# A new order, a float32 fetch and six magnitudes on ScalarE in a fused attention and MLP kernel

## The chip, the cores and the metric

The kernel runs on one core of a Trainium2 chip. A core has five engines that work side by side and meet through semaphores: TensorE (PE; PEld is its loading of weights), VectorE (DVE), ScalarE (ACT), GpSimd (POOL) and SyncE (SP). POOL, SP and ACT can also start transfers (DMAs); what they start runs on 16 shared DMA engines. POOL's transfers can change the type on the way (float32 in memory, bf16 on chip); the transfers that SP and ACT start here move bytes as they are. The metric is device time in microseconds (us) of one launch. The kernel before took 396.82 us (median of three runs, 396.26 to 397.13).

## The reference: what is computed

Eight batches, eight heads, 576 positions, 64 numbers a head, all float32. Every head does masked attention; the first four heads look at the last 32 positions ("local", L in the code), the other four at the positions that are the same modulo 32 ("strided", S). The outputs of all heads stand side by side as 512 numbers for each of 4608 tokens and go through an MLP whose activation is a rational function.

```python
scores = q @ k.T / sqrt(64)
scores = where(mask, scores, -1e9); attn = softmax(scores)
x = (attn @ v) as [4608, 512]
h = x @ w_in                                   # [4608, 2048]
P = a[0] + a[1]*h + a[2]*h**2 + a[3]*h**3
Q = 1 + abs(b[0])*abs(h) + abs(b[1])*h**2
out = (P / (Q + 1e-6)) @ w_out                 # [4608, 512]
```

## The kernel before, in words

Everything on chip is bf16, sums of matmuls are float32 in PSUM, whose eight banks are shared out.

**Attention** goes batch by batch (function `attention`), each in four steps: L heads, S heads, S heads, L heads. A step is: scores on PE, the row maximum on DVE (L805, L887), its subtraction by one more matmul, exp on ACT (L818, L900), a transpose of the result, the product with v on PE (L848, L943), and the division on DVE (L859, L953). Then `turn` transposes the batch's output into XT, which ACT copies out of PSUM (L765). q and k must be transposed too. For batches 0 and 1 (`b < NPE`), `casts` fetches q and k on POOL's queue with conversion to bf16 into an MLP buffer h (L560; two halves n = 0 and n = 1 for L and S heads, q and k each: four transfers a batch), and `loads_pe` transposes them on PE (L623, L660); ACT copies q out of PSUM, DVE copies k (L642 to L674). For batches 2 to 7, POOL writes bf16 copies of q and k to memory, and SP's transposing transfers bring them in; the results of exp are transposed by SP's transfers too (L836, L920).

**The MLP** goes in nine chunks of 512 tokens. `mlp1` makes the 2048 columns of h in two groups of eight tiles: four matmuls a tile (L980), an ACT copy from PSUM into the group's h buffer (L986). Then the activation works on the whole group, 4096 numbers in each of 128 partitions. On DVE, one after the other: z = |h| by clearing the sign bits (L1023), u = b1 z + b0 (L1025), u = u z (L1027). On ACT: u = exp(-ln(u + 1.000001)), the reciprocal of Q (L1051, L1053). On DVE: z = a3 h + a2 (L1054), z = z h (L1056), z = z + a1 (L1057), z = z h (L1058), z = z + a0 (L1059), h = z u (L1060). The first group of chunk 0 is cut in halves (L1003 to L1013), the last group of chunk 8 in smaller pieces, with its magnitude and one step made by ACT (L1019, L1020). `mlp2` multiplies with w_out (L1086), copies out (L1098) and stores (L1105). There are five h buffers, two z and two u buffers, used in turn.

**The order of the work** is not the order of the code. Every operation is recorded with its engine, an assumed duration, a key and the tiles it reads and writes. `schedule` then plays the program forward: at each moment, each engine that is free takes, of the operations whose inputs are ready by the assumed durations, the one with the lowest key. The result is one fixed list for each engine, with semaphore waits between the engines. Keys are in units of tokens: attention of batch b has b*576 and up, the MLP of chunk c has c*512 plus an offset. `QUOTA` says how many PSUM tiles of each kind may be open at once ("ph" are those that the MLP's first matmuls and small transposes write). Where PE would idle at the start or the end, the planner puts in matmuls whose result nobody reads (`filler`, L136). A transfer is assumed to land 2.2 us after its turn, and 9 us later still when it starts after 60 us.

In the planner, an engine is free again when an operation's duration is over, and what depends on it on the same engine can follow at once:

```python
free[e] = t + o.dur
...
lat = 0.0 if u.eng == o.eng else 0.15
u.ready = max(u.ready, o.fin + lat)
```

Of the kernel before, what the change touches and what calls it, by code (L numbers as in the profile page):

```python
# [12 lines left out]
ACT_SET_ID = 6  # L13

# [70 lines left out]
class Prog:  # L85
    QUOTA = {"at": 3, "ph": 3, "sm": 2, "po": 4}
# [64 lines left out]
    def schedule(self):  # L151
# [69 lines left out]
        while left:  # L221
# [45 lines left out]
            for u in o.users:  # L267
                lat = 0.0 if u.eng == o.eng else 0.15
# [101 lines left out]
def bass_strided_sparse_attn__then__act_rational_pade_kernel(nc, q, k, v, moe_w_in, moe_w_out, moe_a, moe_b, out):  # L370
# [7 lines left out]
    HL = H // 2  # L378
# [93 lines left out]
    for dst, srcc in ((IDN, id_c), (ML, ml_c), (MS, ms_c)):  # L472
# [4 lines left out]
         0.1, -1e5, w=[T_co], dma=0.1)  # L477
    P.op("sp", lambda e: e.dma_start(coef[:, 0:4], bass.AP(tensor=pa.tensor, offset=pa.offset, ap=[[0, 128], [1, 4]])),
         0.1, -1e5, w=[T_co], dma=0.1)
    P.op("sp", lambda e: e.dma_start(coef[:, 4:6], bass.AP(tensor=pb.tensor, offset=pb.offset, ap=[[0, 128], [1, 2]])),  # L480
         0.1, -1e5, w=[T_co], dma=0.1)
    T_b.new()
    P.op("dve", lambda e: e.scalar_tensor_tensor(coef[:, 6:8], coef[:, 4:6], -1.0, coef[:, 4:6],
                                                 op0=Alu.mult, op1=Alu.max), 0.2, -1e5, r=[T_co], w=[T_b])
# [58 lines left out]
    def casts(b, after=None):  # L543
        after = after if after else [()] * 7
        key = b * 576 - 1500 if b > 1 else -1e5 + 3e4 * b
# [3 lines left out]
        for n in range(2):  # L549
# [3 lines left out]
            for i, (s_t, d_t, t) in enumerate(((q, q16, T_q[b][n]), (k, k16, T_k[b][n]))):  # L553
# [3 lines left out]
                if b >= NPE:  # L557
                    bulk(s_t, d_t, b, HL * n, HL, H, t, key, after[3 * n + i])
                    continue
# [46 lines left out]
    def loads_pe(b, key, tq, tk, after):  # L606
        for n in range(2):
            h = stage[b, n]
            hv = h.t[:, :, :].rearrange("p g c -> p (g c)")
            for i, (t, st_) in enumerate(((tq, T_q[b][n]), (tk, T_k[b][n]))):  # L610
# [14 lines left out]
                P.op("pe", tr, 1.0, key + 2 * n, r=[st_, h, T_c], w=[sl], after=after)  # L625
# [37 lines left out]
                P.op("pe", tr2, 0.7, key + 1, r=[st_, h, T_c], w=[sw], after=after)  # L663
# [14 lines left out]
    def loads(b, after=(), pace=None):  # L678
        g0, g1, g2 = [[pace[i]] for i in range(3)] if pace else [()] * 3
        key = b * 576 - 20 if b else -700  # L680
# [53 lines left out]
    def turn(b, kind, src, key):  # L734
        for kk in range(2):
# [16 lines left out]
            P.op("pe", tr, 0.5, key, r=[src, T_c], w=[sm])  # L752
# [15 lines left out]
    def attention(b, st):  # L768
# [5 lines left out]
        for kind, idx in (("L", 0), ("S", 0), ("S", 2), ("L", 1)):  # L774
            key = base + 144 * u
# [3 lines left out]
            if kind == "L":  # L779
# [3 lines left out]
                def score(e, tq=tq, tk=tk, sc=sc, idx=idx):  # L783
# [19 lines left out]
                P.op("pe", score, 1.15, key, r=[T_c] + st["TL"], w=[sc])  # L803
# [3 lines left out]
                    1.2, key, r=[sc], w=[ng])  # L807
# [8 lines left out]
                P.op("pe", negm, 0.5, key, r=[ng], m=[sc])  # L816
# [5 lines left out]
                if b < NPE:  # L822
                    for j in range(2):
# [8 lines left out]
                        P.op("pe", trp, 0.5, key, r=[pp, T_c], w=[ph])  # L832
# [20 lines left out]
                P.op("pe", av, 0.8, key, r=[pt] + st["vlr"], w=[acc])  # L853
# [13 lines left out]
            def score(e, tq=tq, tk=tk, idx=idx, sc=sc):  # L867
# [17 lines left out]
            P.op("pe", score, 1.0, key, r=[T_c] + st["TS"], w=[sc])  # L885
# [3 lines left out]
                0.85, key, r=[sc], w=[ng])  # L889

            def negm(e, ng=ng, sc=sc):
# [6 lines left out]
            P.op("pe", negm, 0.4, key, r=[ng], m=[sc])  # L898
# [3 lines left out]
                0.75, key, r=[sc], w=[pp])  # L902
            pt = R_ptS.next()
            if b < NPE:
                for j in range(2):
# [10 lines left out]
                    P.op("pe", trp, 0.4, key, r=[pp, T_c], w=[ph])  # L916
# [31 lines left out]
            P.op("pe", av, 0.5, key, r=[pt, vS], w=[acc])  # L948
# [3 lines left out]
            for x in range(2):  # L952
# [5 lines left out]
                    0.66, key, r=[acc, rc], w=[xsb])  # L958
            if idx:
                turn(b, "S", xsb, base + 500)  # L960
        turn(b, "L", xl, base + 550)
        return land

    def mlp1(c):
        xt = cur_xt[c]
        xc = CH * (c % 3)
        base = c * CH + 1500 if c else 1000
        groups = []
        for g in range(NG):
            h = R_h.next()  # L970
            cut = c == 0 and g == 0
            hf = [Tile(f"hf{i}") for i in range(2)]
            for f in range(g * G, g * G + G):
                ph = PTile("ph", 1)
                key = base + f * 16
# [7 lines left out]
                o = P.op("pe", mm, 0.9, key, r=[xt, T_win[f // G]], w=[ph], after=h.prev)  # L983
                if f == 7:
# [3 lines left out]
                     0.6, key, r=[ph], w=[h, hf[f % G // 4]])  # L988
            key = base + 256 + g * 256
# [7 lines left out]
            def dv(fn, dur, **kw):  # L997
                P.op("dve", fn, dur, key, **kw)
# [16 lines left out]
            else:  # L1015
                if end:
# [4 lines left out]
                         3.7, key, r=[h, T_co], w=[y])  # L1021
                else:
# [33 lines left out]
            dv(lambda e, zz=zz, hh=hh: e.tensor_tensor(zz, zz, hh, op=Alu.mult), tt, r=[h], m=[z])  # L1056
            dv(lambda e, zz=zz: e.tensor_scalar(zz, zz, a_ap[1], None, op0=Alu.add), ts + 0.22, m=[z])  # L1057
            dv(lambda e, zz=zz, hh=hh: e.tensor_tensor(zz, zz, hh, op=Alu.mult), tt, r=[h], m=[z])  # L1058
# [116 lines left out]
```

## Time and profile before

| | |
|---|---|
| runs, us | 397.13, 396.26, 396.82 |
| profiled run, us | 396.87 |
| its span (first to last instruction), us | 395.1 |
| mean granted clock of TensorE | 0.982 |
| matrix multiplications and weight loads | 3859 each |
| DVE instructions | 324 |
| ACT instructions | 316 |
| DMA traffic | 45.76 MB |

A line of the profile names a group of instructions by the kernel's line (L1023 is line 1023), the engine, the operation, what it writes and reads (out<-in) and the shapes; after the bar stand busy us, mean ns of one instruction, and how long the engine was idle just before it and for whom. In the timeline the first number is the start in us, the second the length, and square brackets show idle time before it and what ended it. Instructions of one kind in a row are merged (x2, x16). In a table by stages each engine has its busy time in that stretch and its number of instructions. "SPq" is SP's queue of DMA issues. A matmul's end in the trace is modelled, so PE's busy time is not PE at its peak.

### The profile page before, as it was taken

The page shows a single profiled execution, that of the slowest core. Times are in us where ns is not written, and L with a number is a line of the kernel's source. Part 1 is how long each engine was busy: PE and PEld are TensorE (multiplying, and loading weights), DVE is VectorE, ACT ScalarE, POOL GpSimd, SP SyncE. Part 2 cuts the span into 40 slices and gives each one's busy share as a digit, 9 for nine tenths or more (in the row PEclk, how much of TensorE's full clock was granted, in tenths as well). Part 3 has the DMA queues.
Part 4 walks back from the last instruction along what each step waited for, and adds up shares of the span by engine and source line. Part 5 has one row for each costly group of instructions (what it writes and reads, how often), then busy time and mean ns, then how long its engine had stood idle before and what let it go on. Part 6 is the DMA issues. An engine that isn't in the chain of part 4 may idle for free.

```text
span 395.1 us, 8720 instructions
## 1 busy us (share of the span) xinstructions
PE 358.1 (91%) x3859; PEld 174.5 (44%) x3859; DVE 360.7 (91%) x324; ACT 290.9 (74%) x316; POOL 102.5 (26%) x136
## 2 busy tenths in 40 slices
PE   6889878989999999689989999999899999899695
PEld 2564545344544454344434544444354344344242
DVE  4673999999998999959999999999999999999995
ACT  1356896869387875848696979597968796899971
POOL 8993000640290049004801720001000100101100
PEclk9699999989999999999999999999999999999999
DMA  7999999999599659999999999205300200200202
GB/s 103 175 206 173 215 150 114 122 143 196 161 133 162 129 142 124 124 102 192 141 148 231 146 179 205 51 28 143 60 2 27 81 0 28 81 0 2 106 0 106
DMA packets 129094, 45.76 MB, mean 116 GB/s; under 512 B 116832, under 2 KB 125280, under 8 KB 128864
## 3 DMA queue, kind: packets, MB, share of 16 engines
q0 software_dynamic: 68864, 27.99, 56.8%
q1 hardware_dynamic: 60192, 17.22, 30.6%
q8 instruction: 30, 0.49, 0.5%
q14 instruction: 8, 0.07, 0.1%
HBM read 39.29 MB, written 16.52 MB: 141 GB/s over the span
## 4 chain that ended last, share of the span: by engine, by line
DVE 64%; PE 21%; DMA 7%; issue 4%; ACT 3%; POOL 0%; SPq 0%; POOLq 0%
DVE z L1056 8%; PE PSUM L980 8%; DVE u L1027 8%; DVE h L1060 7%; PE PSUM L1086 7%; DVE z L1058 7%; DVE u L1025 5%; DMA ptS<-pS 5%; DVE z L1057 5%; DVE z L1054 4%; DVE z L1023 4%; DVE z L1059 4%; DVE xS L953 3%; DMA h<-in_q_dram 2%; DVE ng L805 2%
## 5 line engine op out<-in xcount | busy, mean ns | idle before, releaser
L980 PE MATMUL PSUM<-XT,Win 128*128 128x512 bf16 x576 | 135.9, 381 | 12.4 <-ACT h L986 4.5
L1086 PE MATMUL PSUM<-Wout,h 128*128 128x512 bf16 x576 | 135.3, 382 | 6.0 <-DVE h L1060 5.9
L986 ACT ACTIVATE h<-PSUM 128x512 bf16<-128x512 f32 x144 | 82.9, 599 | 40.9 <-PE PSUM L980 40.7
L980 PEld LDWEIGHTS PSUM<-XT,Win 128*128 128x128 bf16 x576 | 51.0, 98 | 80.4 <-ACT h L986 16.5
L1086 PEld LDWEIGHTS PSUM<-Wout,h 128*128 128x128 bf16 x576 | 54.4, 98 | 69.7 <-DVE h L1060 5.8
L1051 ACT ACTIVATE u<-u,consts 128x4096 bf16<-128x4096 bf16 x16 | 59.3, 3709 | 13.1 <-DVE u L1027 12.7
L1105 POOL DMA_DIRECT2D out_dram<-os x32 | 20.9, 656 | 182.5 <-ACT os L1098 182.5
L1053 ACT ACTIVATE u<-u 128x4096 bf16<-128x4096 bf16 x16 | 57.9, 3620 | 0.3
L1027 DVE TENSOR_TENSOR u<-u,z 128x4096 bf16<-128x4096 bf16 x17 | 39.0, 2291 | 0.5
L1058 DVE TENSOR_TENSOR z<-z,h 128x4096 bf16<-128x4096 bf16 x17 | 38.9, 2291 | 0.5
L1056 DVE TENSOR_TENSOR z<-z,h 128x4096 bf16<-128x4096 bf16 x17 | 38.9, 2287 | 0.4
L1060 DVE TENSOR_TENSOR h<-z,u 128x4096 bf16<-128x4096 bf16 x17 | 38.8, 2283 | 0.4
L573 POOL DMA_DIRECT2D vL<-in_v_dram x32 | 27.4, 886 | 0.0
L1098 ACT ACTIVATE os<-PSUM 128x512 f32<-128x512 f32 x34 | 19.2, 605 | 10.8 <-PE PSUM L1086 10.5
L524 POOL DMA_DIRECT2D q<-in_q_dram x6 | 5.3, 888 | 83.9 <-DMA tk<-k 83.9
L765 ACT ACTIVATE XT<-PSUM 128x576 bf16<-128x576 bf16 (+2 forms) x40 | 19.4, 563 | 9.8 <-PE PSUM L749 6.0
L1025 DVE TENSOR_SCALAR u<-z,coef 128x4096 bf16<-128x4096 bf16 x17 | 22.8, 1344 | 0.5
L953 DVE TENSOR_TENSOR xS<-PSUM,rc 100x512 bf16<-100x512 f32 x32 | 20.5, 683 | 2.9 <-PE PSUM L943 2.6
L1057 DVE TENSOR_SCALAR z<-z,coef 128x4096 bf16<-128x4096 bf16 x17 | 22.3, 1312 | 0.5
L1059 DVE TENSOR_SCALAR z<-z,coef 128x4096 bf16<-128x4096 bf16 x17 | 21.8, 1280 | 0.3
L1054 DVE TENSOR_SCALAR z<-h,coef 128x4096 bf16<-128x4096 bf16 x16 | 21.7, 1354 | 0.4
L1023 DVE TENSOR_SCALAR z<-h 128x4096 uint16<-128x4096 uint16 x16 | 19.5, 1220 | 2.4 <-ACT h L986 2.4
(87 smaller groups left out, 388.4 us busy)
## 6 DMA issues: line engine op xcount, KB each, us to landing
out_dram<-os POOLq DMA_DIRECT2D x32, 256.0 KB, 3.6
q<-in_q_dram POOLq DMA_DIRECT2D x12, 288.0 KB, 8.0
k<-in_k_dram POOLq DMA_DIRECT2D x12, 288.0 KB, 9.1
vL<-in_v_dram POOLq DMA_DIRECT2D x32, 96.0 KB, 10.5
vS<-in_v_dram POOLq DMA_DIRECT2D x16, 144.0 KB, 10.1
Win<-in_moe_w_in_dram POOLq DMA_DIRECT2D x8, 256.0 KB, 12.6
Wout<-in_moe_w_out_dram POOLq DMA_DIRECT2D x4, 512.0 KB, 23.9
h<-in_q_dram POOLq DMA_DIRECT2D x4, 288.0 KB, 13.5
```

The costliest lines, as they stand in the source:

```text
L980: r = e.matmul(ph.f, Win[:, kk, f * 128:(f + 1) * 128], XT[:, kk, xc:xc + CH], start=(kk == 0), stop=(kk == NK1 - 1))
L986: P.op("act", lambda e, f=f, ph=ph, h=h: e.activation(h.t[:, f % G, :], ph.f, AF.Copy), 0.6, key, r=[ph], w=[h, hf[f % G // 4]])
L1025: dv(lambda e, zz=zz, uu=uu: e.tensor_scalar(uu, zz, b1_ap, b0_ap, op0=Alu.mult, op1=Alu.add), ts + 0.28, r=[z, T_b], w=[u])
L1027: dv(lambda e, zz=zz, uu=uu: e.tensor_tensor(uu, uu, zz, op=Alu.mult), tt, r=[z], m=[u])
L1051: P.op("act", lambda e, uu=uu: e.activation(uu, uu, AF.Ln, bias=eps1, scale=1.0), 0.833 * W / 1000 + 0.28, key, r=[T_co], m=[u])
L1053: P.op("act", lambda e, uu=uu: e.activation(uu, uu, AF.Exp, scale=-1.0), 0.833 * W / 1000 + 0.19, key, m=[u])
L1056: dv(lambda e, zz=zz, hh=hh: e.tensor_tensor(zz, zz, hh, op=Alu.mult), tt, r=[h], m=[z])
L1057: dv(lambda e, zz=zz: e.tensor_scalar(zz, zz, a_ap[1], None, op0=Alu.add), ts + 0.22, m=[z])
L1058: dv(lambda e, zz=zz, hh=hh: e.tensor_tensor(zz, zz, hh, op=Alu.mult), tt, r=[h], m=[z])
L1059: dv(lambda e, zz=zz: e.tensor_scalar(zz, zz, a_ap[0], None, op0=Alu.add), ts + 0.22, m=[z])
L1060: dv(lambda e, zz=zz, hh=hh, uu=uu: e.tensor_tensor(hh, zz, uu, op=Alu.mult), tt, r=[z, u], m=[h])
L1086: r = e.matmul(po.f, h.t[:, j, m * 128:(m + 1) * 128], Wout[:, kk, :], start=(kk == 0), stop=(kk == NF - 1))
```

## The change: what it does

1. *The planner's model.* A VectorE operation keeps its engine for 0.083 us less than its duration, an ACT operation for 0.11 less (`OVER`); an operation that depends on one of the same engine is ready 0.035 (DVE) or 0.03 us (ACT) after its end (`OWN`). Late transfers are assumed to land after 7.2 us more instead of 9. Many assumed durations are changed, PE's above all; four PSUM tiles of kind "ph" may be open instead of three.
2. *Keys.* The MLP's keys lie later against attention's (1737 in place of 1500 for its first half, 2611 in place of 2250 for its second), the second half of the activation on DVE has a later key than the first, and attention's four steps and the turns are spaced differently. The absolute value of b (L483) moves from the front of DVE's list to key 100.
3. *Float32 fetch.* The first q and the first k (batch 0, L heads) are no longer fetched on POOL's queue with conversion. ACT starts two plain float32 transfers into a z and a u buffer that the MLP does not use yet, and DVE converts them to bf16 with one copy each. The load of ACT's function table is attached to ACT's first operation that is not a transfer.
4. *Magnitudes.* For the second group of chunks 2 to 7, z = |h| is made by ACT in four pieces of two tiles (1024 columns) each, a piece as soon as its two tiles are copied, in place of the one DVE instruction over all eight.

```diff
+OVER = {"dve": 0.083, "act": 0.11}
+OWN = {"dve": 0.035, "act": 0.03}
...
-    QUOTA = {"at": 3, "ph": 3, "sm": 2, "po": 4}
+    QUOTA = {"at": 3, "ph": 4, "sm": 2, "po": 4}
...
-            free[e] = t + o.dur
+            free[e] = t + max(o.dur - OVER.get(e, 0.0), 0.05)
...
-                o.fin = dmafree[e] + 2.2 + (9 if t > 60 else 1.5 if t > 12 else 0.0)
+                o.fin = dmafree[e] + 2.2 + (7.2 if t > 60 else 0.8 if t > 12 else 0.0)
...
-                lat = 0.0 if u.eng == o.eng else 0.15
+                lat = OWN.get(o.eng, 0.0) if u.eng == o.eng else 0.15
...
-                                                 op0=Alu.mult, op1=Alu.max), 0.2, -1e5, r=[T_co], w=[T_b])
+                                                 op0=Alu.mult, op1=Alu.max), 0.2, 100, r=[T_co], w=[T_b])
...
-        key = b * 576 - 1500 if b > 1 else -1e5 + 3e4 * b
+        key = b * 576 - 1343 if b > 1 else -1e5 + 3e4 * b
...
+                if b == 0 and n < 1:
+                    sg = (R_z.tiles + R_u.tiles)[2 * n + i].new()
+                    sv = sg.t.bitcast(f32)[0:TP, :, :].rearrange("p g c -> p (g c)")
+                    ho = hv[0:TP, i * HL * TW:(i + 1) * HL * TW]
+                    P.op(('act', 'act', 'sp', 'sp')[2 * n + i], lambda e, s_t=s_t, sv=sv, n=n: e.dma_start(
+                        sv.rearrange("p (h c) -> p h c", c=TW),
+                        bass.AP(tensor=s_t.tensor, offset=s_t.offset + (b * H + HL * n) * S * D,
+                                ap=[[TW, TP], [S * D, HL], [1, TW]])),
+                        0.45 if n else 0.2, (-3e6 if n == 0 else -5e5) + 2 * n + i, w=[sg], dma=1.5)
...
+                        P.op("dve", lambda e, ho=ho, sv=sv: e.tensor_copy(ho, sv), 1.22, -710 + 2 * n + i,
+                             r=[sg], w=[t], after=h.prev)
+                    continue
...
-            key = base + 144 * u
+            key = base + 144 * u + (0, -80, -170, 96)[u]
...
-                turn(b, "S", xsb, base + 500)
-        turn(b, "L", xl, base + 550)
+                turn(b, "S", xsb, base + 753)
+        turn(b, "L", xl, base + 628)
...
-        base = c * CH + 1500 if c else 1000
+        base = c * CH + 1737 if c else 949
...
-                key = base + f * 16
+                key = base + f * 16.4
...
-            key = base + 256 + g * 256
+            key = base + 339 + g * 229
...
+                elif c >= 2 and g:
+                    for i in range(4):
+                        P.op("act", lambda e, zi=z.t[:, 2 * i:2 * i + 2, :], hi=h.t[:, 2 * i:2 * i + 2, :]:
+                             e.activation(zi, hi, AF.Abs), 1.05333, key + 0, r=[hp[i]], w=[z])
...
-            dv(lambda e, zz=zz, hh=hh: e.tensor_tensor(zz, zz, hh, op=Alu.mult), tt, r=[h], m=[z])
+            dv(lambda e, zz=zz, hh=hh: e.tensor_tensor(zz, zz, hh, op=Alu.mult), tt, r=[h], m=[z], off=109)
...
-            dv(lambda e, zz=zz, hh=hh, uu=uu: e.tensor_tensor(hh, zz, uu, op=Alu.mult), tt, r=[z, u], m=[h])
+            dv(lambda e, zz=zz, hh=hh, uu=uu: e.tensor_tensor(hh, zz, uu, op=Alu.mult), tt, r=[z, u], m=[h], off=152)
...
-        base = c * CH + 2250
+        base = c * CH + 2611
...
-    first = P.order["act"][0]
+    first = next(o for o in P.order["act"] if o.dma is None)
```

More of the change, by code (lines that the diff above doesn't have):

```diff
@@ L679, in loads @@
         g0, g1, g2 = [[pace[i]] for i in range(3)] if pace else [()] * 3
-        key = b * 576 - 20 if b else -700
+        key = b * 576 - 32 if b else -700
         st = {}
@@ L982, in mm @@
                     return r
-                o = P.op("pe", mm, 0.9, key, r=[xt, T_win[f // G]], w=[ph], after=h.prev)
+                o = P.op("pe", mm, 0.875, key, r=[xt, T_win[f // G]], w=[ph], after=h.prev)
                 if f == 7:
@@ L1093, in mlp2 @@
             o = R_o.next()
-            key = base + 300 if last else base + m * 60
+            key = base + 300 if last else base + m * 77
             if last and m % 2:
```

53 lines of the change are left out of this document (29 added, 24 removed).

## The prediction

> **What bounds the kernel now.** I read the page's first two parts, then the busy table by stages, the waits of VectorE (DVE), the chain that ended last, the groups of instructions and the timeline of both ends. First the page: busy times, and the span in 40 slices.
>
> ```profile
> span 395.1 us, 8720 instructions
> ...
> PE 358.1 (91%) x3859; PEld 174.5 (44%) x3859; DVE 360.7 (91%) x324; ACT 290.9 (74%) x316; POOL 102.5 (26%) x136
> ...
> DVE  4673999999998999959999999999999999999995
> ```
>
> DVE is full from the fifth slice on. The busy table by stages (length; then PE, PEld, DVE, ACT, POOL busy with instruction counts; clock; DMA):
>
> ```profile
> 37.00:130.00 93.00, 84.19 (x1127) 43.87 (x1125) 89.67 (x85) 71.20 (x86) 23.42 (x26) 0.98 1.29 157
> 130.00:176.00 46.00, 40.33 (x527) 19.78 (x526) 41.56 (x39) 31.92 (x34) 13.33 (x15) 1.00 1.21 124
> 176.00:295.00 119.00, 113.17 (x1320) 54.67 (x1317) 116.90 (x99) 93.47 (x105) 26.46 (x34) 1.00 0.89 128
> 295.00:374.50 79.50, 73.75 (x348) 31.78 (x345) 78.09 (x47) 69.21 (x62) 7.44 (x12) 1.00 0.10 38
> ```
>
> From 37 to 374.5 us DVE works 326.2 of 337.5 us. Of its 11.3 idle us, 6.6 are the six stalls after the first of this list, the rest small steps. From the timeline, the stalls (idle time and releaser in brackets):
>
> ```profile
> 37.27 0.69 DVE L1003 TENSOR_SCALAR z<-h 128x2048 uint16<-128x2048 uint16 x1 [6.26 <-ACT h L986]
> ...
> 40.72 0.69 DVE L1003 TENSOR_SCALAR z<-h 128x2048 uint16<-128x2048 uint16 x1 [0.65 <-ACT h L986]
> ...
> 127.25 1.23 DVE L1023 TENSOR_SCALAR z<-h 128x4096 uint16<-128x4096 uint16 x1 [1.29 <-ACT h L986]
> ...
> 169.83 0.26 DVE L950 RECIPROCAL rc<-PSUM 100x16 f32<-100x16 f32 x1 [1.02 <-PE PSUM L930]
> 172.05 1.29 DVE L953 TENSOR_TENSOR xS<-PSUM,rc 100x512 bf16<-100x512 f32 x2 [1.96 <-PE PSUM L943]
> 174.41 1.23 DVE L1023 TENSOR_SCALAR z<-h 128x4096 uint16<-128x4096 uint16 x1 [1.07 <-ACT h L986]
> ...
> 211.65 1.29 DVE L953 TENSOR_TENSOR xS<-PSUM,rc 100x512 bf16<-100x512 f32 x2 [0.65 <-PE PSUM L943]
> ```
>
> The first is the head: before 37 us there is no MLP work for DVE. The three from 169 on (4.05 us) are one event, shown below. The small steps, from the timeline of the tail:
>
> ```profile
> 340.44 2.29 DVE L1060 TENSOR_TENSOR h<-z,u 128x4096 bf16<-128x4096 bf16 x1
> 342.64 1.22 DVE L1023 TENSOR_SCALAR z<-h 128x4096 uint16<-128x4096 uint16 x1
> 343.90 1.35 DVE L1025 TENSOR_SCALAR u<-z,coef 128x4096 bf16<-128x4096 bf16 x1
> 345.28 2.29 DVE L1027 TENSOR_TENSOR u<-u,z 128x4096 bf16<-128x4096 bf16 x1
> ...
> 358.50 1.22 DVE L1023 TENSOR_SCALAR z<-h 128x4096 uint16<-128x4096 uint16 x1
> ...
> 384.02 7.07 PE L1086 MATMUL PSUM<-Wout,h 128*128 128x512 bf16 x32
> ```
>
> L1023, which needs nothing of L1060, starts 0.09 us before L1060's end (342.64 against 342.73). L1025, which needs L1023, starts 0.04 us after its end. So a dependent neighbour costs 0.12 us more than an independent one. One MLP group takes 358.50 - 342.64 = 15.86 us of DVE.
>
> **The change, part by part.** Durations are means of these groups (busy, mean ns, idle before):
>
> ```profile
> L986 ACT ACTIVATE h<-PSUM 128x512 bf16<-128x512 f32 x144 | 82.9, 599 | 40.9 <-PE PSUM L980 40.7
> L1051 ACT ACTIVATE u<-u,consts 128x4096 bf16<-128x4096 bf16 x16 | 59.3, 3709 | 13.1 <-DVE u L1027 12.7
> L1053 ACT ACTIVATE u<-u 128x4096 bf16<-128x4096 bf16 x16 | 57.9, 3620 | 0.3
> ...
> L1098 ACT ACTIVATE os<-PSUM 128x512 f32<-128x512 f32 x34 | 19.2, 605 | 10.8 <-PE PSUM L1086 10.5
> ...
> L1023 DVE TENSOR_SCALAR z<-h 128x4096 uint16<-128x4096 uint16 x16 | 19.5, 1220 | 2.4 <-ACT h L986 2.4
> ...
> L1034 ACT ACTIVATE u<-u 128x2048 bf16<-128x2048 bf16 x2 | 3.8, 1910 | 0.1
> ...
> L1019 ACT ACTIVATE z<-h 128x4096 bf16<-128x4096 bf16 x1 | 3.6, 3617 | 0.0
> ...
> L1007 DVE TENSOR_TENSOR u<-u,z 128x2048 bf16<-128x2048 bf16 x2 | 2.5, 1225 | 0.1
> ```
>
> *Magnitudes.* Second groups of chunks 2 to 7: six L1023 leave DVE, each worth 1.26 us of chain (343.90 - 342.64) where it depends, 1.14 where it overlaps. I take 1.17: 6 x 1.17 = -7.0 us, between -7.6 and 0 (ScalarE may become the bound). ScalarE (ACT) gains 24 pieces of 1024: L1034 and L1053 give 0.835 ns an element and 0.20 us fixed, so 1.055 us a piece, 4.2 a group, 25.3 in all; its 290.9 us become about 316. A piece that waits for its z buffer holds the evictions (L986) behind it, and with them PE's banks. With two z buffers in turn, z has so far been free since one group earlier.
>
> That is cheap while attention lasts: from 176 to 295 us ACT is busy 93.5 of 119. In the tail (295 on) it is 69.2 of 79.5. There a pair of groups costs ACT 16 x 0.599 + 2 x (3.709 + 3.620) + 4 x 0.605 = 26.7 us; with one set of pieces 30.9, less perhaps 1.8 where its instructions overlap. DVE's pair falls from 31.7 to at best 31.7 - 1.17 - 14 steps x 0.12 = 28.9. So the two are level there, and I give back 2.0 us over the 2.5 pairs of the tail (between 0 and 2.5 x (30.9 - 28.9) = 5).
>
> *Order.* The planner's new model lets a VectorE instruction start 0.083 us before the last one ends, and a dependent one only 0.035 after; so when a group's next step isn't ready it takes one of another group or of attention. Off the stalls, 11.3 - 6.6 = 4.7 us of DVE idle at 0.036 each (tail: 79.50 - 78.09 = 1.41 us, 40 steps) are some 130 dependent steps. All turned would give 130 x 0.12 = 15.6 us, none 0. I take somewhat under half, 7.0: two z and two u buffers allow two groups in flight, but a group whose magnitudes come from ACT is late, and its partner then runs alone. The Trainium skill, "VectorE: DVE Perf Modes", section "The DRAIN you can't avoid", says that the next instruction doesn't start until the pipe is empty, and that eight copies took 13.88 us with or without semaphores between them. By that the term would be 0; here the trace disagrees, with 342.64 against 342.73.
>
> The planner's shorter DMA latencies, the turns' and MLP's later keys, and the fourth "ph" bank move work without adding instructions. The stalls at 127 and 169 us could go and others come: -1.0 us, between -6.6 and the first rival below. The last chunk's output steps (374.5 on) hold the same instructions: 0.
>
> *Head.* From the timeline, the first fetches and who waits for them:
>
> ```profile
> 1.34 0.89 POOL L560 DMA_DIRECT2D h<-in_q_dram  x1 [0.89 <-POOLq L1160]
> ...
> 1.90 0.91 DVE L495 MEMSET vS<- 128x1024 uint32 x1
> ...
> 2.23 0.74 POOL L560 DMA_DIRECT2D h<-in_k_dram  x1
> ...
> 8.69 0.69 PE L623 MATMUL PSUM<-IDN,h 72*128 72x72 bf16 x16 [1.78 <-DMA h<-in_q_dram]
> ...
> 10.66 0.16 DVE L483 SCALAR_TENSOR_TENSOR coef<-coef 128x2 f32<-128x2 f32 x1 [4.97 <-DMA coef<-in_moe_b_dram]
> ...
> 10.68 0.69 PE L623 MATMUL PSUM<-IDN,h 72*128 72x72 bf16 x16 [0.76 <-DMA h<-in_k_dram]
> ...
> 12.89 1.12 PE L623 MATMUL PSUM<-IDN,h 72*128 72x72 bf16 x16 [0.99 <-DMA h<-in_q_dram]
> ...
> 14.66 1.16 PE L623 MATMUL PSUM<-IDN,h 72*128 72x72 bf16 x16
> ```
>
> SP's stores at the end, by the DMA issues (KB each, median us to landing):
>
> ```profile
> out_dram<-os SPq DMA_DIRECT2D x4, 256.0 KB, 2.4
> ```
>
> Four fetches on POOL's queue are used one every 2 us: at 8.7, 10.7, 12.9 and 14.7. Now the first two go out on ACT's queue, unconverted: 72 x 2048 x 4 B = 576 KB each; ACT issues them ahead of its table load, when it has nothing else to do. SP's float32 stores of 256 KB land in 2.4 us; 1152 KB at twice to four times that is 5 to 10 us, so they land at 6 to 11. The other two, now first on POOL's queue, land near 8.7 to 10.7 alone, 10.7 to 14.7 beside the float32. DVE adds two casts: no row shows one; L1003 (0.69) and L1027 (2.29) bound it, and I take L1007's 1.225, which reads as many bytes. They lie in DVE's idle time as long as L483, which waited 4.97 us for coefficients, stands behind them; its key moves it there. What is late next are the steps from the transposes to 37.27, which stay. POOL issues two fetches fewer, so v and the weights start about 1.6 us sooner. Gain 2.5 us, between -4.0 (10.7 instead of 14.7) and +2.4 (nothing lands sooner, both casts stand behind).
>
> Sum: -2.5 - 7.0 + 2.0 - 7.0 - 1.0 = -15.5; 395.1 becomes 379.6. The profiled run took 396.87 us, 1.8 beside its span, and the median of the runs is 396.82, the same. So about 381.4, said as 381 us.
>
> **The rivals.** *DMA latency (the other side).* The planner now believes late transfers 1.8 us quicker. From the chain and the SP issues:
>
> ```profile
> 150.77 18.63 DMA ptS<-pS
> ...
> ptS<-pS SPq DMA_TRANSPOSE x12, 5.0
> ```
>
> This one took 18.6 us where the median is 5.0; it made the 4.05 us stall. If such a miss came in every one of the six batches whose transposes go by DMA, 6 x 4.05 = 24 us, less the one there is: 20 - 15.5 = about +5, 401 us. It decides from four more stalls (16 us) on. For it: less margin in the plan. Against it: one such stall in twelve transfers now, and attention is planned further ahead of the MLP.
>
> *ScalarE becomes the bound.* If z is only free when both groups in flight end, ACT stands in front of its pieces and the evictions behind wait. Then the magnitudes gain nothing (-7.0 and +2.0 go: +5.0), and a tail paced by ACT at 30.9 us a pair loses some 1.5 us of overlap: 381.4 + 6.5, about 388. It decides once ACT needs more than DVE's 28.9 a pair. For it: 69.2 of 79.5 busy. Against: ACT idles 40.7 us for L980 alone.
>
> *The order does nothing.* Dependent steps stay as they are: 381.4 + 7 = 388. For it: two buffers only. Against: L1023 overlaps already, at 342.64. On the side of this rival stands the rule on the DRAIN named above.
>
> *The casts hold POOL's queue.* In the head POOL issues fetches without a pause (from 1.34 on). If it can't while DVE casts, its later fetches shift by up to 2 x 1.2 us, the head gains nothing, and the time is 381.4 + 2.5 = 384. For it: the second q and k still come that way. Against: DVE's memsets in the head ran beside POOL's issues, which took 0.89 and 0.74 us. The Trainium skill, "SBUF — State Buffer", section "SBUF: two separate sides" (the "DVE blocks DMA" trap), says this of float32 copies in SBUF: GpSimd is locked out and can't write descriptors. No run here shows it so far.
>
> *Full overlap.* 110 of the 130 steps turn, and the 127 and 169 us stalls go: 381.4 - 6 - 4 = 371. Against: PE needs 128 matmuls of 7.07 / 32 = 0.22 us, 28.3 us, for each pair of groups, close behind.
>
> **How the numbers follow.** Forecast 0.44, full overlap 0.15, order nothing 0.11, ScalarE 0.10, casts 0.06, DMA latency 0.14. All but the last are faster; of the last, 0.12 ends slower and 0.02 within 0.2% (0.8 us, about what a measurement can tell from no change). The likeliest case's own range is 375 to 387. The range reaches to full overlap below and into the DMA case above: 370 to 394. Faster 0.86, same 0.02, slower 0.12.
>
> **What would show it.** Six L1023 fewer on DVE and 24 pieces near 1.05 us on ACT; ACT near 316 us busy. In the tail, DVE steps of two groups in turn, each starting 0.08 before the last ends, and a pair of groups near 29 to 30 us. First DVE work of the MLP near 35. DVE's busy time near 350 (360.7 - 7 - 60 overlaps x 0.08 + 2.4 = 351). Wrong it would be by DVE stalls on PE behind DMA transposes, by ACT full in the tail while DVE idles, or by transposes of the first q later than 8.7.

## The result and the profile after

The changed kernel took 386.78 us (median of 4 runs, 384.94 to 387.88) against 396.98 us for the kernel before (4 runs, 396.26 to 398.25). The ratio is 0.9701 (95% interval 0.9659 to 0.9744): 10.2 us faster, 5.8 us above the forecast of 381. The profiled run took 386.40 us, 1.8 more than its span. In some runs of this study the chip was disturbed; the ratios leave those out, medians do not.

In the changed kernel the lines stand lower in the code: L980 is now L999, L986 L1005, L1003 L1022, L1023 L1046, L1025 L1048, L1060 L1083, L1086 L1109; the attention's L848 is L866, L943 and L930 are L961 and L948, L836 and L920 are L854 and L938; the pieces are L1044, the casts L575. In the experiments that substitute lists, lines lie one to eight further on (L1028 is L1022). The diffs of the experiments are shortened.

The first part of the page after:

```profile
span 384.6 us, 8677 instructions
...
PE 348.1 (90%) x3800; PEld 179.4 (47%) x3850; DVE 347.3 (90%) x320; ACT 308.4 (80%) x340; POOL 101.4 (26%) x134
```

The busy table by stages of after, columns as in the prediction (the tail now ends at 364):

```profile
37.00:130.00 93.00, 82.15 (x1152) 44.52 (x1162) 90.23 (x86) 74.32 (x92) 22.93 (x26) 0.98 1.39 151
130.00:176.00 46.00, 43.57 (x529) 22.84 (x520) 45.79 (x42) 43.09 (x47) 12.25 (x15) 1.00 1.27 139
176.00:295.00 119.00, 108.98 (x1297) 56.67 (x1315) 107.53 (x95) 99.08 (x113) 26.67 (x34) 0.97 0.95 126
295.00:364.00 69.00, 68.60 (x313) 30.91 (x319) 68.75 (x41) 67.19 (x60) 6.88 (x11) 1.00 0.11 41
```

In the tail DVE is busy 68.75 of 69 us, PE 68.60 and ACT 67.19: three engines full at once. From 176 to 295 DVE is idle 11.5 of 119 us, where it was idle 2.1 before. From the groups of after, the magnitudes (24 pieces on ACT, ten instructions left on DVE):

```profile
L1044 ACT ACTIVATE z<-h 128x1024 bf16<-128x1024 bf16 x24 | 25.1, 1063 | 1.0 <-DVE h L1083 0.7
...
L1046 DVE TENSOR_SCALAR z<-h 128x4096 uint16<-128x4096 uint16 x10 | 12.3, 1229 | 0.0
```

The timeline of DVE in the tail of after shows the steps of two groups in turn:

```profile
313.03 2.28 DVE L1083 TENSOR_TENSOR h<-z,u 128x4096 bf16<-128x4096 bf16 x1
315.23 1.28 DVE L1082 TENSOR_SCALAR z<-z,coef 128x4096 bf16<-128x4096 bf16 x1
316.43 1.22 DVE L1046 TENSOR_SCALAR z<-h 128x4096 uint16<-128x4096 uint16 x1
317.56 2.28 DVE L1083 TENSOR_TENSOR h<-z,u 128x4096 bf16<-128x4096 bf16 x1
319.77 1.34 DVE L1048 TENSOR_SCALAR u<-z,coef 128x4096 bf16<-128x4096 bf16 x1
...
346.49 2.29 DVE L1083 TENSOR_TENSOR h<-z,u 128x4096 bf16<-128x4096 bf16 x1
```

L1082 at 315.23 starts 0.08 us before L1083 ends (315.31). Two L1083 further on (339.64 and 346.49) a pair of groups has taken 346.49 - 317.56 = 28.9 us, where two groups took 31.7 before. The stalls in the timeline of after (idle time and releaser in brackets):

```profile
38.58 0.69 DVE L1022 TENSOR_SCALAR z<-h 128x2048 uint16<-128x2048 uint16 x1 [6.24 <-ACT h L1005]
...
181.91 0.22 DVE L875 RECIPROCAL rc<-PSUM 128x10 f32<-128x10 f32 x1 [4.11 <-PE PSUM L866]
...
185.57 0.22 DVE L875 RECIPROCAL rc<-PSUM 128x10 f32<-128x10 f32 x1 [1.57 <-PE PSUM L866]
...
249.16 0.26 DVE L968 RECIPROCAL rc<-PSUM 100x16 f32<-100x16 f32 x1 [2.73 <-PE PSUM L948]
...
255.63 1.35 DVE L1048 TENSOR_SCALAR u<-z,coef 128x4096 bf16<-128x4096 bf16 x1 [1.65 <-ACT z L1044]
...
379.80 0.69 DVE L1119 COPY os<-PSUM 128x512 f32<-128x512 f32 x1 [3.17 <-PE PSUM L1109]
```

The first MLP work on DVE comes at 38.58, not earlier than before (37.27) but 1.3 us later. The stalls near 180 and 250 us, behind the attention's matmuls, are new; so is one of 1.65 us behind ACT's pieces (L1044), which no experiment explains. The chain of waits of after, between 160 and 260 us, says what these stood behind:

```profile
169.60 11.49 DMA ptL<-pL
...
232.85 15.88 DMA ptS<-pS
```

Both are SP's transposing transfers.

**An account of the difference.** DVE's work from its first MLP step on can be summed over its instructions, one by one: when that step starts, the durations of its steps (those that overlap counted in full), the gaps under 0.3 us between neighbours (negative where they overlap), the stalls over 0.3 us, and what lies behind its last step. The five make the span, but for rounding. (The expectations count rows of the timeline, where neighbours of one kind are merged, and so name fewer steps.) Beside the two kernels stand runs that the next section tells of.

| us | first step | steps | gaps (overlapping / all others under 0.3) | stalls | rest | span |
|---|---|---|---|---|---|---|
| before | 37.3 | 353.1 | -6.3 (138 / 138) | 7.8 | 3.3 | 395.1 |
| after | 38.6 | 344.2 | -15.8 (220 / 50) | 14.4 | 3.2 | 384.6 |
| order alone | 37.0 | 351.5 | -15.6 (221 / 57) | 8.4 | 3.2 | 384.5 |
| without the overlap model | 42.2 | 345.4 | -4.5 (124 / 142) | 10.1 | 3.2 | 396.4 |
| overlap model alone | 37.2 | 352.9 | -12.0 (187 / 87) | 17.9 | 3.2 | 399.3 |
| latency 9 | 40.7 | 344.5 | -12.0 (185 / 79) | 31.9 | 3.2 | 408.4 |
| best | 36.9 | 344.8 | -15.9 (220 / 50) | 9.6 | 3.2 | 378.7 |

From before to after: head +1.3, steps -8.9, gaps -9.5, stalls +6.6, in sum -10.5. The order gives what the change gives; the magnitudes' gain and the loss in stalls and head nearly cancel.

### The profile page after: what moved, and what is told of

Its sections match the earlier page's. It is cut to its first block, busy times and chain, and to the rows that moved or that the text cites. A ratio compares the mean times of both kernels' runs of the same rounds, so it can differ in the third digit from the quotient of the medians.

```text
span 384.6 us, 8677 instructions
## 1 busy us (share of the span) xinstructions
PE 348.1 (90%) x3800; PEld 179.4 (47%) x3850; DVE 347.3 (90%) x320; ACT 308.4 (80%) x340; POOL 101.4 (26%) x134
## 4 chain that ended last, share of the span: by engine, by line
DVE 47%; PE 29%; DMA 10%; ACT 9%; issue 4%; ACTq 0%
PE PSUM L1109 11%; PE PSUM L999 10%; DVE u L1050 6%; DVE h L1083 5%; DVE z L1081 5%; DVE z L1079 5%; DMA ptS<-pS 4%; ACT u L1074 3%; DVE u L1048 3%; DMA ptL<-pL 3%; DVE xS L971 3%; DVE z L1080 3%; DVE ng L823 3%; DMA z<-in_k_dram 3%; DVE z L1077 3%
## 5 line engine op out<-in xcount | busy, mean ns | idle before, releaser
L999 PE MATMUL PSUM<-XT,Win 128*128 128x512 bf16 x552 | 130.6, 382 | 7.3 <-ACT XT L783 1.7
L1109 PE MATMUL PSUM<-Wout,h 128*128 128x512 bf16 x553 | 129.8, 383 | 4.3 <-issue 2.1
L1005 ACT ACTIVATE h<-PSUM 128x512 bf16<-128x512 f32 x144 | 81.5, 616 | 28.2 <-PE PSUM L999 28.1
L999 PEld LDWEIGHTS PSUM<-XT,Win 128*128 128x128 bf16 x576 | 54.7, 98 | 70.0 <-ACT XT L783 2.5
L1109 PEld LDWEIGHTS PSUM<-Wout,h 128*128 128x128 bf16 x576 | 54.8, 99 | 65.8 <-DVE h L1083 2.6
L1083 DVE TENSOR_TENSOR h<-z,u 128x4096 bf16<-128x4096 bf16 x17 | 38.8, 2283 | 0.2
L1079 DVE TENSOR_TENSOR z<-z,h 128x4096 bf16<-128x4096 bf16 x17 | 38.6, 2270 | 0.1
L1121 ACT ACTIVATE os<-PSUM 128x512 f32<-128x512 f32 x34 | 20.3, 606 | 12.8 <-PE PSUM L1109 12.8
L1044 ACT ACTIVATE z<-h 128x1024 bf16<-128x1024 bf16 x24 | 25.1, 1063 | 1.0 <-DVE h L1083 0.7
L1048 DVE TENSOR_SCALAR u<-z,coef 128x4096 bf16<-128x4096 bf16 x17 | 22.8, 1340 | 1.7 <-ACT z L1044 1.6
L1082 DVE TENSOR_SCALAR z<-z,coef 128x4096 bf16<-128x4096 bf16 x17 | 22.0, 1297 | 0.3
L823 DVE TENSOR_REDUCE ng<-PSUM 128x10 bf16<-128x960 f32 x16 | 18.0, 1149 | 2.1 <-PE PSUM L813 2.0
```

What stands on the lines that cost most here:

```text
L999: r = e.matmul(ph.f, Win[:, kk, f * 128:(f + 1) * 128], XT[:, kk, xc:xc + CH], start=(kk == 0), stop=(kk == NK1 - 1))
L1005: P.op("act", lambda e, f=f, ph=ph, h=h: e.activation(h.t[:, f % G, :], ph.f, AF.Copy), 0.6, key, r=[ph], w=[h, hf[f % G // 4], hp[f % G / ...
L1048: dv(lambda e, zz=zz, uu=uu: e.tensor_scalar(uu, zz, b1_ap, b0_ap, op0=Alu.mult, op1=Alu.add), ts + 0.28, r=[z, T_b], w=[u])
L1083: dv(lambda e, zz=zz, hh=hh, uu=uu: e.tensor_tensor(hh, zz, uu, op=Alu.mult), tt, r=[z, u], m=[h], off=152)
L1109: r = e.matmul(po.f, h.t[:, j, m * 128:(m + 1) * 128], Wout[:, kk, :], start=(kk == 0), stop=(kk == NF - 1))
```

## Experiments

Theory: overlap and magnitudes are each worth some 7 to 10 us, the float32 fetch costs, and the stalls come from late transposing transfers. Rivals: the time comes from one part alone; the head waits for the masks; the stalls come from the shorter assumed latency, from the order of SP's queue, or from other traffic.

### The fetch and the magnitudes, taken back on the same order

To leave every list as the changed plan has it, operations are exchanged after planning.

**e1_pool_fetch**

```diff
     P.schedule()
+    # the two ACT transfers and the two DVE casts leave their lists;
+    # POOL's converting transfers stand first in POOL's
+    P.order["act"].remove(ld); P.order["dve"].remove(c)
+    P.order["pool"][0:0] = [q, k]
```

> The changed kernel's order on every engine is kept; only the first q and k go back to POOL's queue with conversion (first in that queue), the two ACT transfers and the two DVE casts are gone. Theory (the float32 fetch is what made the head later: more bytes in flight, the masks and the second q and k land later): first transposes back near 8.7 us instead of 11.1, the first MLP work on DVE (the first half of |h| of chunk 0) at 37 us or before instead of 38.6, time 385 us or less. Rival (the head is set by the new order of PE and its filler matmuls, not by the fetch): first MLP work stays at 38.6, time 386.8.

**e2_mag_dve**

```diff
     P.schedule()
+    # the four pieces of a group become one DVE instruction,
+    # just ahead of the first that reads it
+    for x in ops: P.order["act"].remove(x)
+    o.eng = "dve"; P.order["dve"].insert(at, o)
```

> The changed kernel's order is kept; only the six magnitudes go back to one DVE instruction each, put just ahead of the step that needs them. Theory (each is worth its 1.15 us of DVE, and ScalarE has just about the room): 386.8 + 6 x 1.1 = 393 us. Rival (ScalarE is the bound where they run, so they gain nothing): 386.8 us or less, with ScalarE's busy share in the tail falling from 97% and DVE's staying.

**e3_order_only**: both edits at once, so that only the order is left.

> The changed kernel's order with both other parts undone (fetch by POOL, magnitudes on DVE). What is left of the gain over the kernel before is that of the order. Theory: e1 and e2 add up, 393 - 2 = 391 us, so the order alone gains about 6 us of 397. Rival (the order does nothing without the magnitudes moved): 397 us.

Measured, beside 398.03 us before (11 runs, 396.21 to 403.79): e1 385.05 us (ratio 0.9603, 0.9546 to 0.9659); e2 393.58 us (0.9749, 0.9686 to 0.9813); e3 386.34 us (0.9704, 0.9652 to 0.9757). The page of e3:

```profile
PE 348.0 (90%) x3800; PEld 178.3 (46%) x3850; DVE 352.1 (92%) x324; ACT 288.3 (75%) x316; POOL 104.3 (27%) x136
```

Nothing but the order is changed in e3, and its ratio is that of the whole change (0.9704 and 0.9701). By the account, magnitudes and fetch together take 7.3 us off the steps and 0.2 off the gaps, and give it back: +1.6 in the head and +6.0 in stalls. The ratios of e1 and e2 lean the way of the theory (without the float32 fetch 1% better, without the pieces 0.5% worse), but their intervals touch or overlap after's. The theories of e2 (6.6 us over after) and e3 (391 us) did not come: e2 loses a third of that by the ratio, and the order alone gains more than was expected of it. The timeline of e1 still has a stall near 180, though a smaller one:

```profile
180.57 0.22 DVE L881 RECIPROCAL rc<-PSUM 128x10 f32<-128x10 f32 x1 [2.95 <-PE PSUM L872]
```

### The head: what the first transposes wait for

The timeline of the head in after (rows of DVE and PE):

```profile
7.41 1.22 DVE L575 CAST h<-z 72x2048 bf16<-72x2048 f32 x1 [1.82 <-DMA z<-in_q_dram]
...
11.07 1.12 PE L641 MATMUL PSUM<-IDN,h 72*128 72x72 bf16 x16 [3.18 <-DMA MS<-c_ms]
...
12.08 1.22 DVE L575 CAST h<-z 72x2048 bf16<-72x2048 f32 x1 [3.45 <-DMA z<-in_k_dram]
...
13.36 1.14 PE L641 MATMUL PSUM<-IDN,h 72*128 72x72 bf16 x16 [0.29 <-DVE h L575]
...
15.71 1.86 PE L138 MATMUL PSUM<-FL 128*128 128x512 bf16 x4 [0.33 <-issue]
...
17.41 0.69 PE L641 MATMUL PSUM<-IDN,h 72*128 72x72 bf16 x16
```

and the DMA issues of its first 14 us (KB each, us to landing):

```profile
ML<-c_ml SPq DMA_DIRECT2D x1, 120.0 KB, 6.3
MS<-c_ms SPq DMA_DIRECT2D x1, 72.0 KB, 9.3
...
IDN<-c_idn SPq DMA_DIRECT2D x1, 32.0 KB, 2.8
```

In the kernel before, these three take 2.1, 2.6 and 1.7 us. e1, with the same lists but POOL's fetch, has q and k earlier:

```profile
8.21 0.69 PE L647 MATMUL PSUM<-IDN,h 72*128 72x72 bf16 x16 [1.50 <-DMA h<-in_q_dram]
...
10.55 0.69 PE L647 MATMUL PSUM<-IDN,h 72*128 72x72 bf16 x16 [1.12 <-DMA h<-in_k_dram]
```

Its second q is transposed at 13.90, and its MLP work starts at 37.49, 1.1 us before after's. One such pair says little: the six kernels with this order and POOL's fetch (e1, e3, e7, e9, e10, e11) start it at 35.81 to 38.48, the four with the float32 fetch (after, e2, e4, e12) at 38.58 to 40.37. The two groups only just do not meet, but their means, 37.2 and 39.4, say that the fetch costs.

In after, q lands at 7.4 and is cast at 8.6, but its transposes start at 11.07, behind the masks, with which the identity shares a semaphore. **e4_idn_alone** gives the identity its own:

```diff
     T_c.new()
+    T_m = Tile("masks").new()
...
-             0.1, -1e6, w=[T_c], dma=0.3)
+             0.1, -1e6, w=[tc], dma=0.3)      # IDN: T_c; ML, MS: T_m
...
-r=[T_c] + st["TL"]
+r=[T_c, T_m] + st["TL"]
```

> The changed kernel; the first transposes wait only for the identity matrix, the scores for the masks as well (one semaphore for the three constants becomes two). Theory (the late mask transfer, which ended PE's wait at 11.07 us, only hides the late k and the late second q): first transposes near 8.7 us, but the first MLP work still at 38 to 38.6 us, time 386 to 387. Rival (the wait for the masks is what costs the head): first MLP work near 36.3 us, time 384.5.

Measured 387.9 us (ratio 0.9759, 0.971 to 0.9809), no better than after. The timeline of its head (the second fence row is k, the third the second q):

```profile
8.79 0.69 PE L642 MATMUL PSUM<-IDN,h 72*128 72x72 bf16 x16 [1.35 <-DVE h L576]
...
14.02 1.14 PE L642 MATMUL PSUM<-IDN,h 72*128 72x72 bf16 x16 [4.00 <-DVE h L576]
...
18.08 1.17 PE L642 MATMUL PSUM<-IDN,h 72*128 72x72 bf16 x16
```

q is transposed 2.3 us sooner, k and the second q 0.7 later, and MLP work starts at 40.37. So the masks are not what costs: with q early, PE waits 4.00 us for k. The second q is not late by itself. In after it lands at 13.12 (issued at 1.33, 11.8 us to landing; before it was 12.76), but PE's fixed list has it behind k's transposes and the four filler matmuls of L138 at 15.71. What costs, as far as these rows show, is k.

### The model of overlap, taken out and alone

**e5_no_overlap_model** is after, planned anew:

```diff
-OVER = {"dve": 0.083, "act": 0.11}
-OWN = {"dve": 0.035, "act": 0.03}
+OVER = {}
+OWN = {}
```

> The changed kernel planned again without the overlap in the planner's model (an instruction keeps its engine for its whole duration, a dependent one can follow at once, as before); keys, durations, quotas, fetch and magnitudes are those of the change. Theory (the order gains by putting independent neighbours on DVE): overlapping steps fall from some 180 to near the 110 of the kernel before, dependent ones rise from 46 to over 100, and the time goes up by 70 x 0.12 = 8 us, to 395. Rival (the gain comes from the keys and durations, the overlap is by the way): 387 us.

**e6_overlap_model_alone** is before with these lines and the two that use them, and nothing else of the change.

> The kernel before with nothing but the overlap put into its planner's model. Theory: overlapping DVE steps rise by some 70, worth 8 us: 397 - 8 = 389 us, if no new stalls come. Rival (without the new keys and durations it does nothing or harms): 397 us or more.

Measured, beside 397.03 us before (17 runs): e5 399.82 us (12 runs, ratio 1.006, 1.0031 to 1.0089); e6 403.06 us (1.0146, 1.0117 to 1.0176). Both are slower than before. In e5's tail a group's steps follow on one another again, each 0.04 us after the last one's end:

```profile
307.24 1.29 DVE L1080 TENSOR_SCALAR z<-z,coef 128x4096 bf16<-128x4096 bf16 x1
308.56 2.29 DVE L1081 TENSOR_TENSOR z<-z,h 128x4096 bf16<-128x4096 bf16 x1
```

By the account its gaps are 11.3 us longer than after's and its head 3.6, its stalls 4.3 shorter. The 11.3 is what overlap is worth, measured by taking it away; the theory had 8. In e6 the model turns 49 steps (138 to 187) and wins 5.7 us of gaps, but loses 10.1 in stalls, from its timeline:

```profile
127.27 1.16 DVE L807 TENSOR_REDUCE ng<-PSUM 128x10 bf16<-128x960 f32 x1 [4.04 <-PE PSUM L797]
```

With before's keys, durations, quota and latency the attention around 130 us comes late. The model pays only with the new ones, and these only with the model.

### The stalls near 180 and 250

**e8_latency_9** tests the prediction's rival, the shorter assumed latency (after, planned anew with before's figures):

```diff
-(7.2 if t > 60 else 0.8 if t > 12 else 0.0)
+(9 if t > 60 else 1.5 if t > 12 else 0.0)
```

> The changed kernel planned again with the late transfers' landing assumed 9 us and 1.5 us later, as before, instead of 7.2 and 0.8. If the shorter latency is what costs (stalls on transfers that the plan thinks landed): DVE's stalls between 39 and 295 us fall from 11 us to under 5, time 381 us. If it does not (the stalls come from how the queues meet, and the longer latency only delays what waits): stalls stay, time 387 us or more.

Measured 409.47 us (1.0297, 1.0266 to 1.0328). The longer latency makes the plan 22.7 us worse than after, above all by stalls, the longest of them from its timeline:

```profile
189.33 1.23 DVE L1046 TENSOR_SCALAR z<-h 128x4096 uint16<-128x4096 uint16 x1 [9.78 <-ACT h L1005]
```

So a longer assumption does not cure the stalls. It makes another plan, though, so it doesn't show where after's stalls come from; the next runs do, on after's lists. **e7_pt_first** is e1 with SP's list changed: where the transposes of pL stand directly behind a q or k transpose that a later batch needs, they move ahead of it (two places).

```diff
+    sp = P.order["sp"]
+    for i in range(len(sp)):
+        j = i
+        while sp[j].dst.name[:2] == "pt" and sp[j-1].dst.name[:2] in ("tq", "tk") and sp[j-1].dst.name[-1] == "S":
+            sp[j-1], sp[j] = sp[j], sp[j-1]
+            j -= 1
```

> The kernel of e1 (changed order, first fetch by POOL) with three entries of SP's list moved: where a transpose of exp's result (pL) stands directly behind the transpose of a later batch's q or k for the S heads, it goes in front of it. Theory (the DVE stall near 180 us, 3 to 4 us, comes from the pL transposes queued behind a q transpose that takes 7 to 9 us to issue): that stall goes, time 3 us under e1, 382 us beside 385. Rival (the transfers themselves are late, whatever their place): the stall stays within 1 us, time as e1.

Measured 381.59 us (0.9582, 0.9542 to 0.9621; e1's interval overlaps it). The stall near 180 is still there (3.71 us): the theory's time came, but not by its cause. SP's queue in the timeline of e7:

```profile
162.22 12.01 SPq L860 DMA_TRANSPOSE ptL<-pL  x2
```

In e1 they stand at 169.61 and their issue takes 6.31 us; here it begins 7.4 us sooner and takes 5.7 longer. So it isn't what stands in front of them on SP's queue. **e9_v_later** changes POOL's list instead (on e1): v of batches 5 and 7, which is needed much later, is fetched behind three and two more output stores.

```diff
+    for g, st in ((3, ("stos0", 3)), (4, ("stos3", 4))):
+        vs = [o for o in po if o.dst.name in ("vsvL1", "vS1") and o.gen == g]
+        ...                              # taken out of POOL's list
+        po[at + 1:at + 1] = vs           # and put behind the store st
```

> The kernel of e1 (changed order, first fetch by POOL) with the v fetches of batches 5 and 7 moved back in POOL's list, behind three and two output stores; everything else in place. Theory (the transposes behind the stalls near 180 and 250 us are slow because they share the DMA engines with POOL's fetch of v in packets of 128 bytes): the stalls near 180 (3 us) and 250 us (1.4 us) shrink by at least half, time 2 to 4 us under e1's 385. Rival (it is SP's own queue, which takes 4 to 9 us for each transpose whatever else runs): stalls and time as e1.

Measured, beside 396.96 us before (11 runs): 383.83 us (0.9634, 0.9594 to 0.9674), no better than e1. The timelines of SP's and POOL's queues, first after:

```profile
146.47 1.36 POOL L587 DMA_DIRECT2D vL<-in_v_dram  x1
147.82 3.08 POOL L591 DMA_DIRECT2D vL<-in_v_dram  x4
150.89 1.82 POOL L598 DMA_DIRECT2D vS<-in_v_dram  x2
...
162.11 7.45 SPq L707 DMA_TRANSPOSE tq<-q  x1
169.60 9.46 SPq L854 DMA_TRANSPOSE ptL<-pL  x2
```

then e9:

```profile
159.92 1.37 SPq L713 DMA_TRANSPOSE tq<-q  x1
161.33 4.45 SPq L860 DMA_TRANSPOSE ptL<-pL  x2
...
176.98 3.77 POOL L597 DMA_DIRECT2D vL<-in_v_dram  x4
...
186.69 3.74 POOL L597 DMA_DIRECT2D vL<-in_v_dram  x4
...
214.95 0.26 DVE L974 RECIPROCAL rc<-PSUM 100x16 f32<-100x16 f32 x1 [6.22 <-PE PSUM L954]
```

With v out of the way the same transposes are issued in 1.37 and 4.45 us in place of 7.45 and 9.46, and DVE doesn't stall near 180 nor near 250. In after the seven v fetches land between 159.18 and 175.47, just while these transposes are issued. All six kernels with this order and v in its old place (after, e1 to e4, e7) stall near 180, by 2.13 to 5.21 us at the longest wait; the four with v moved (e9 to e12) do not. That is the cause of the stall near 180: POOL's v fetches, still in the DMA engines, slow SP's transposes. Near 250 the same is not shown: e3, with v in its old place, has no stall there either. And two sets of v now follow each other (176.98, 186.69), and behind them stands a slow transpose in e9's chain of waits:

```profile
196.40 18.09 DMA ptS<-pS
```

The stall has moved to 214.95, and takes back what was won. The same cause there is argued from the order of the rows; no run takes that v away.

**e10_v_later_pt_first** is e9 with e7's order of SP's list.

> e9 with the pL transposes also in front of the S heads' q transpose, as in e7. Theory: with the v fetches gone from that stretch, the pL transposes land by 170 us and the stall near 180 goes altogether, time 379 to 381 us. Rival: as e7, a stall of 3.7 us near 180, 381.6 us.

Measured 379.69 us (0.9533, 0.9504 to 0.9562), the best of all, 17.3 us under before by the medians of that chip. The longest stall of its middle, from its timeline:

```profile
211.95 0.26 DVE L974 RECIPROCAL rc<-PSUM 100x16 f32<-100x16 f32 x1 [2.88 <-PE PSUM L954]
```

As the theory has it, there is no stall near 180, but that one had gone with e9 already. What falls here is the one near 212, from 6.22 us to 2.88; why SP's order does that is open.

### The two other parts, on the version with few stalls

**e11_mag_dve_again** is e10 with e2's edit, **e12_f32_again** e10 with after's float32 fetch and casts.

> e10 with the six magnitudes back on DVE (as in e2), to size that part where transfers disturb least. Theory: 6 x 1.1 us of DVE come back, time 5 to 7 us over e10. Rival (ScalarE's load takes it back): within 2 us of e10.

> e10 with the changed kernel's float32 fetch by ACT and its two casts on DVE put back, to size that part where transfers disturb least. Theory: the first MLP work on DVE comes at 38.5 to 40 us instead of 37 to 38.5, time 1 to 3 us over e10. Rival (the fetch makes no difference): within 1 us.

Measured: e11 389.72 us (0.974, 0.9699 to 0.9781), e12 380.87 us (0.9597, 0.956 to 0.9634). Against e10's 0.9533, the pieces on ACT are worth (0.974 - 0.9533) x 396.96 = 8.2 us here, and their intervals lie apart; DVE's busy time differs by 352.9 - 345.6 = 7.3. In the other pairs the same part is worth 4.0 us (e3 against e1) and 1.9 (e2 against after), with intervals that overlap. The float32 fetch costs (0.9597 - 0.9533) x 396.96 = 2.5 us by the ratios, 1.2 by the medians, and the intervals just touch; its sign is that of the head, where e12's first MLP step comes at 38.65 and e10's at 36.91. e12's two casts start at 6.88 and 11.62, like after's. e12 is also after itself with nothing but the v fetches and three entries of SP's list moved: (0.9701 - 0.9597) x 397 = 4.1 us, and these intervals lie apart.

## Why the prediction was right, and where it was off

The sign and the likeliest case, between the full overlap and the order that does nothing, came out, and 386.8 lies in the range, at the upper end of the likeliest case's own (375 to 387). The time alone doesn't tell this case from the rivals at 384 and 388; the counts and the experiments do. Of the signs of being wrong, two came: stalls behind DMA transposes, and transposes of the first q later than 8.7 (11.07). The sum was -15.5, the account gives -10.5:

- **Magnitudes, -7.0: right.** The count and the duration (24 pieces of 1.063 us) are as forecast, ACT is busy 308.4 and not 316 (its own overlaps weren't taken off), the magnitudes on DVE went from 19.5 to 12.3 us. All steps together fell 8.9: the rest are steps that got slightly shorter, and e3, which has no pieces, shows 1.5 of that.
- **The +2.0 given back in the tail: not seen.** ACT is busy 67.19 of 69 us there, level with DVE, but a pair of groups takes 28.9 us, which was the best value that DVE allowed.
- **Order, -7.0: right in mechanism, too small.** 82 more steps overlap (138 to 220), the others fell from 138 to 50, and the gaps by 9.5 us; taking the model out makes them 11.3 longer. I took under half of 130 steps; it was 88, about two thirds. e3 puts the order by itself at 10.6 us (a span of 384.5 for 395.1). The Trainium skill, "VectorE: DVE Perf Modes", section "The DRAIN you can't avoid", by which this term was 0, doesn't hold for these neighbours: at 315.23 one starts 0.08 us early. That section itself points on to "Two Vector instructions with no wait between them", by which an instruction that isn't held starts earlier; the trace agrees with that. So the rival that had this rule on its side (the order does nothing) falls, by e3 too.
- **Head, -2.5: wrong in sign, +1.3.** The step "they land at 6 to 11" gave q and k (7.4 and 12.1; the latter is over it), but I costed the float32 as if nothing else moved. It moves 1152 KB over the same DMA engines, where the converting issues list 576: the mask MS took 9.3 us to land where it took 2.6, k is transposed at 13.36 where it was at 10.68, the second q, behind k on PE's list, at 17.41 where it was at 12.89. That the bytes are the reason is argued; that it comes with the fetch, the two groups of kernels above show. The two POOL fetches saved didn't show either; why stands at the casts below. e12 against e10 leans the same way with nothing else changed: 1.7 us later. The Trainium skill, "DMA: Bandwidth & Descriptors", section "Issuing engines are not separate DMA queues", says that what different engines start runs interleaved on the same 16 DMA engines; these rows agree.
- **Stalls, -1.0: wrong, +6.6.** Of these, 2.0 stand at the end (3.17 in place of 1.20 at the last wait for L1109); e3, e1 and e10 have that wait too, so it belongs to the order; why it came is open. The rest is the middle, where the prediction named the place (DVE behind DMA transposes) and put it in the rival on DMA latency, with another mechanism. e8 shows that a longer assumed latency is no cure, e7 that SP's order isn't it near 180, e9 that POOL's v fetches are.

With the head at +1.3 and the stalls at +6.6, and the other terms as predicted less the 2.0, the sum would have been -7.0 - 7.0 + 1.3 + 6.6 = -6.1; the larger overlap (-2.5) and the steps (-1.9, most of it those that got shorter) make -10.5. So the nearness to the forecast is partly two errors of opposite sign.

**The other rivals.** ScalarE isn't the bound: the tail has DVE and PE as full as ACT, and taking its pieces back costs 8.2 us in e11, where this rival has them gain nothing. Casts that hold POOL's queue: its mechanism is there, though small. The timeline of POOL in after, with the casts at 7.41 and 12.08:

```profile
6.68 2.09 POOL L598 DMA_DIRECT2D vS<-in_v_dram  x2
8.75 5.21 POOL L609 DMA_DIRECT2D Win<-in_moe_w_in_dram  x8
```

and in e10, which has no casts:

```profile
8.09 1.30 POOL L604 DMA_DIRECT2D vS<-in_v_dram  x2
9.33 4.36 POOL L615 DMA_DIRECT2D Win<-in_moe_w_in_dram  x8
```

The two groups of issues that a cast meets take 0.79 and 0.85 us longer. In each, one issue alone is long: those at 7.31 and 11.95 take 1.46 and 1.48 us and end 0.14 and 0.13 us after the cast does. In all six kernels here that cast the groups take 1.87 to 2.19 and 4.97 to 5.23 us, in all eight that don't (before among them) 1.30 to 1.32 and 4.35 to 4.38. Together that is 1.6 us in after, as much as the two fetches fewer should have gained, so Win is all issued at 13.96 instead of 13.69. The Trainium skill, "SBUF — State Buffer", section "SBUF: two separate sides" (the "DVE blocks DMA" trap), says that a float32 copy on DVE keeps GpSimd from writing descriptors; the trace agrees, with 0.8 us for each cast of 1.22. As a rival for the time (384) it doesn't decide, since the head's loss lies at k, which is fetched past POOL; the second q behind it was issued ahead of the casts.

## What to carry to other kernels

A model of an engine's overlap, and the priorities, durations and limits that go with it, are one change: each alone made this kernel slower than it was (1.5% and 0.6%), together they made it 3% faster. Before a fetch is moved to a faster-looking queue, count the bytes that share the DMA engines with it, and what small transfers stand beside it. When an urgent transfer is late, look at what other queues have in flight: moving the v fetches and three entries of SP's list, on top of the old fetch, gained another 7.1 us by the medians (386.78 to 379.69); the lists alone (e12) 4.1 by the ratios.

## What the runs showed of the hardware that was not expected

Two transposes (tq, then ptL x2) issued on SP's queue in 1.37 and 4.45 us with no v fetch in flight, and in 7.45 and 9.46 us behind seven v fetches on POOL's queue that had been issued 10 to 16 us before the first of them, and were still landing. Here a transfer on one queue so slows the issue on another, long after its own issue. The kernel before has it too: a transpose of q issued at 156.32, beside v fetches issued from 148 to 157, takes 7.63 us. A 120 KB constant took 6.3 us and a 72 KB one 9.3 us to land beside two float32 transfers of 576 KB, a 32 KB one, issued in the same moment as the first of the two, 2.8; in the kernel before, without such transfers, they took 2.1, 2.6 and 1.7. And 0.12 us between a dependent and an independent neighbour, which looks like nothing in one row, was 9.5 of 395 us.
